# A fused mLSTM-attention and MLP kernel: from the fourth chunk a step's weighing and the next step's scores become one block on TensorE, with a cheaper set-up and a new table of order

## The chip, the cores and the metric

The kernel runs on one core of a Trainium2 chip. The metric is the device time of one launch in microseconds. The inputs lie in HBM in a layout that the host prepared; everything below happens in one program on the core's engines: PE (TensorE, matmuls and transposes), DVE (VectorE), ACT (ScalarE), POOL (GpSimd) and SP (SyncE, which here only issues DMAs).

## The reference, cut to what matters

```python
# attention, per batch and head (4 batches x 8 heads, 768 tokens, head size 40)
for t in range(S):
    m_new  = max(f_gate[t] + m, i_gate[t])
    f_stab = exp(f_gate[t] + m - m_new);  i_stab = exp(i_gate[t] - m_new);  m = m_new
    C = f_stab * C + i_stab * outer(v[t], k[t])
    n = f_stab * n + i_stab * k[t]
    y[t] = sigmoid(o_gate[t]) * (C @ q[t]) / max(abs(n . q[t]), 1.0)
# MLP on the 3072 tokens (320 wide, 2048 hidden)
x = y laid out as 3072 x 320
h = x @ w_in
g = h * erf(softplus(h))
return g @ w_out
```

All data is float32. Products of the MLP are made from high and low halves (three products for most of `h`, three for most of the output), so that TensorE's faster float32 form keeps enough bits.

## The kernel before, in words

**Tiling.** The 768 tokens are cut into 12 chunks of 64. A chunk has two *steps*, r = 0 and r = 1, each of two of the four batches with all their heads. The matrix C and the vector n live in `state[r]`, one tile for each r, which a chunk's step reads and then updates. After both steps of a chunk its 256 rows of y are transposed and go through the MLP in four *groups* `mlp(g)`, 48 in all: each group takes 512 of the 2048 hidden units.

**A step on PE** has these blocks, all into `pa` tiles in PSUM, of which there are two: *scores* (L626, k times q, 16 matmuls in the program); *state part* (L635, `qe` times `state`); *key/value part* (L640, the addition to the state); *heads* (L649, the weighted scores `dm` times v, which ends the step's output). In the program the scores, the state part and the heads are 16, 16 and 32 instructions; the trace counts each of them twice. The transposes of the chunk before (L510, three for each step) share the scores' tile. From chunk `JOIN` = 3 on, one planned operation holds transposes, state part, key/value part and scores; the heads come later as an operation of their own, when DVE has multiplied the scores into `dm` (L681). Behind the heads DVE makes the divisor (L710 to L712), the output (L718, L724), a copy of 64 columns of it that the third transpose needs (L725), and the new state (L730, L732).

**A group on PE**: 32 up matmuls into two `h` tiles (L858, products `xh,wh`, `xl,wh` and for two thirds `xh,wl`), later the down matmuls into the two halves of `pob`: L915 for the first six groups, which are not split, and L917, L919 and L920 for the others. Between them ACT copies h (L866), runs softplus and erf (L870, L874) with a change of its table before each (L985), and DVE multiplies (L878) and forms the low half `gl` (L894). When the four groups of a chunk are summed up, ACT copies each half of `pob` to `o` (L925), from where it is stored. The next chunk's first down matmuls write the same `pob` tile, and wait for that copy.

**Opening.** POOL makes masks and constants (`one`, `ident`, `keep`, L347 to L384) and `sel` (L362 to L370), which says for each partition which gate it holds. DVE's first instruction (`heads_of`, L379) and ACT's work on `one` (L375) need `sel`. DVE then runs the gate scans (L432 to L450) and splits the weights as they arrive (L740, L751, L753, L767, L805). The inputs qk, kvo, w_in (two halves of 512 KB each for several parts), w_out and the gates are issued by SP.

**What sets the order.** All operations are handed to a `Plan`, which lists them with costs and due times (`FIRST_DUE`, `EVERY`, `STEPS`, plus a table `SHIFT` with a number for each operation) and replays them with a model of the engines; on each engine the ready operation with the earliest due time is next. The resulting order is the program's order, engine by engine; waits are only for data and for buffers. The model also counts PE's instructions in blocks of `BLOCK`, and holds up an operation that would cross into a block before `FETCH` microseconds have gone by; where it foresees a gap on PE it puts in filler matmuls on `ident` (`stay`, L983).

## Time and profile before

| what | us |
|---|---|
| runs before, median (lowest to highest), 3 runs | 481.37 (480.41 to 481.48) |
| the profiled execution | 479.99 |
| its span (first to last instruction) | 478.3 |
| mean granted clock of TensorE | 0.993 |
| last output copy starts | 474.28 |

The profiled execution is 1.7 us longer than its span, and 1.38 us shorter than the median of the runs. In the lines of the profile, times are microseconds from the span's start. "L858" is line 858 of the kernel before; "[0.53 <-ACT o L925]" means that the engine stood idle for 0.53 us, and that the last thing it waited for was ACT's instruction of that line. "x8" is the number of instructions drawn into one row; "128*128" is the part of the array that a matmul uses. In the windows view a row gives, for each engine, its busy time in the stretch and the number of instructions, then the granted clock, the busy share of the DMA engines and the bytes that they moved.

### The profile page before, as it was taken

The numbers are of one execution on the slowest core, as the hardware profiler recorded it, in microseconds if no ns is written. First come the engines' busy times: TensorE is split into PE (matmuls) and PEld (weight loads), VectorE is DVE, ScalarE is ACT, GpSimd is POOL, SyncE is SP. The second block draws the span as 40 slices with busy tenths as digits, with TensorE's granted clock in tenths as the row PEclk, the third lists the DMA queues.
The fourth block names the chain that finished last, engine by engine and source line by source line (L and its number), as shares of the span: only waits on it lengthen the run. The fifth ranks groups of instructions, "written<-read, shape, count | busy, mean of one in ns | idle before, by whom it ended". The sixth has DMA issues, their size and how long they took to land.

```text
span 478.3 us, 14687 instructions
## 1 busy us (share of the span) xinstructions
PE 456.3 (95%) x6482; PEld 421.5 (88%) x6482; DVE 322.0 (67%) x574; ACT 313.6 (66%) x433; POOL 48.2 (10%) x71
## 2 busy tenths in 40 slices
PE   6788999899999999999999999999999999999996
PEld 2457878678999999999899999999999999999985
DVE  4889999999988378367639557769069551554280
ACT  3636799948598399648179288396287272894760
POOL 4000002101203003002101101104003100000000
PEclk9979999999999999999999999999999999999999
DMA  8997835332362433033324313604040300000011
GB/s 282 313 307 224 270 123 170 105 116 78 115 169 66 134 128 129 18 116 107 93 108 128 104 29 108 171 14 143 7 127 21 116 16 1 2 14 15 1 27 29
DMA packets 42476, 50.77 MB, mean 106 GB/s; under 512 B 22700, under 2 KB 27308, under 8 KB 42412
## 3 DMA queue, kind: packets, MB, share of 16 engines
q1 hardware_dynamic: 42412, 49.83, 34.6%
q8 instruction: 51, 0.84, 0.7%
q14 instruction: 13, 0.11, 0.1%
HBM read 45.68 MB, written 4.13 MB: 104 GB/s over the span
## 4 chain that ended last, share of the span: by engine, by line
PE 82%; DVE 8%; ACT 7%; issue 2%; POOL 1%; POOLq 0%; ACTq 0%; DVEq 0%
PE h L858 35%; PE pob L919 10%; PE pob L917 10%; PE pob L920 9%; PE pa L649 3%; PE pob L983 3%; PE pa L635 2%; PE pa L626 2%; PE pob L915 2%; PE pa L915 2%; ACT L985 2%; DVE raw L751 1%; PE pa L510 1%; PE pa L640 1%; ACT n L870 1%
## 5 line engine op out<-in xcount | busy, mean ns | idle before, releaser
L858 PE MATMUL h<-xh,wh 128*128 128x256 f32 x576 | 159.6, 288 | 0.0
L858 PE MATMUL h<-xl,wh 128*128 128x256 f32 x576 | 156.7, 283 | 0.0
L858 PEld LDWEIGHTS h<-xh,wh 128*128 128x128 f32 x576 | 110.0, 191 | 1.9 <-ACT hb L866 0.6
L858 PEld LDWEIGHTS h<-xl,wh 128*128 128x128 f32 x576 | 110.2, 191 | 0.7 <-DVE vg L614 0.2
L866 ACT ACTIVATE hb<-h 128x512 f32<-128x512 f32 x96 | 56.4, 593 | 81.9 <-PE h L858 81.8
L858 PE MATMUL h<-xh,wl 128*128 128x256 f32 x384 | 108.6, 283 | 0.1
L919 PE MATMUL pob<-woh,gh 128*128 128x320 f32 x328 | 99.4, 315 | 1.6 <-ACT o L925 1.6
L920 PE MATMUL pob<-wo,gh 128*128 128x320 f32 x328 | 97.5, 309 | 0.0
L878 DVE TENSOR_TENSOR n<-n,hb 128x1024 f32<-128x1024 f32 x48 | 58.7, 1231 | 40.9 <-ACT n L874 40.8
L985 ACT ACT_TABLE_LOAD x61 | 78.3, 1283 | 1.8 <-PEq L1038 0.8
L604 POOL TENSOR_SCALAR_AFFINE_SELECT dm<-dm 128x512 f32<-128x512 f32 (+1 forms) x40 | 42.5, 1069 | 322.6 <-ACT dm L583 321.3
L858 PEld LDWEIGHTS h<-xh,wl 128*128 128x128 f32 x384 | 73.4, 191 | 0.3 <-DVE wl L767 0.3
L919 PEld LDWEIGHTS pob<-woh,gh 128*128 128x128 f32 x328 | 61.6, 188 | 3.5 <-ACT o L925 2.4
L917 PE MATMUL pob<-woh,gl 128*128 128x320 f32 x328 | 61.0, 314 | 1.8 <-ACT o L925 1.6
L920 PEld LDWEIGHTS pob<-wo,gh 128*128 128x128 f32 x328 | 61.6, 188 | 0.0
L894 DVE TENSOR_TENSOR gl<-n,gh 128x1024 fp32r<-128x1024 f32 x42 | 52.1, 1245 | 2.0 <-ACT gh L888 1.0
L917 PEld LDWEIGHTS pob<-woh,gl 128*128 128x128 f32 x328 | 50.4, 188 | 3.4 <-ACT o L925 2.4
L870 ACT ACTIVATE n<-hb 128x1024 f32<-128x1024 f32 x48 | 50.6, 1058 | 1.2
L874 ACT ACTIVATE n<-n 128x1024 f32<-128x1024 f32 x48 | 49.5, 1053 | 0.2
L710 DVE TENSOR_SCALAR den<-pa 128x8 f32<-128x8 f32 x24 | 3.9, 161 | 46.8 <-PE pa L649 45.8
L925 ACT ACTIVATE o<-pob 128x320 f32<-128x320 f32 x22 | 9.3, 435 | 32.6 <-PE pob L917 26.3
L681 DVE TENSOR_TENSOR dm<-pa,dm 128x512 f32<-128x512 f32 x24 | 16.5, 687 | 20.0 <-PE pa L626 17.3
(94 smaller groups left out, 537.0 us busy)
## 6 DMA issues: line engine op xcount, KB each, us to landing
qk<-in_qk_dram SPq DMA_DIRECT2D x24, 512.0 KB
kvo<-in_kvo_dram SPq DMA_DIRECT2D x24, 484.0 KB
raw<-in_w_out_dram SPq DMA_DIRECT2D x16, 320.0 KB
dm<-gd SPq DMA_DIRECT2D x40, 128.0 KB
raw<-in_w_in_dram SPq DMA_DIRECT2D x8, 512.0 KB
out_dram<-o SPq DMA_DIRECT2D x48, 80.0 KB
eT<-gd SPq DMA_DIRECT2D x22, 128.0 KB
eT<-gd SPq DMA_DIRECT2D x22, 80.0 KB
```

What stands on the lines that cost most here:

```text
L604: nc.gpsimd.affine_select(out=x, in_=x, pattern=[[0, H], [1, L]], compare_op=ALU.is_ge, fill=0.0, base=base, channel_multiplier=-1)
L858: nc.tensor.matmul(h[:, n * T:(n + 1) * T], w, m, start=(s == 0), stop=(s == len(ops) - 1))
L866: nc.scalar.activation(G('hb')[:, hs], G(f'h{i}'), AF.Copy)
L870: nc.scalar.activation(new('n0', [128, 1024], ('n0', g)), G('hb'), AF.Softplus)
L874: nc.scalar.activation(G('n0'), G('n0'), AF.Erf)
L878: nc.vector.tensor_tensor(G('n0'), G('n0'), G('hb'), op=ALU.mult)
L894: nc.vector.tensor_tensor(new('gl', [128, 1024], ('gl', g), F32R), G('n0'), G('gh').bitcast(F32), op=ALU.subtract)
L915: nc.tensor.matmul(acc(b), G('n0')[:, ts], t['wo', j], start=(j == 0), stop=(j == NFF - 1))
L917: nc.tensor.matmul(acc(b), G('gl')[:, ts], woh[:, j], start=False, stop=(j == NFF - 1))
L919: nc.tensor.matmul(acc(b), G('gh')[:, ts], woh[:, j], start=(j == 0), stop=False)
L920: nc.tensor.matmul(acc(b), G('gh')[:, ts], t['wol', j], start=False, stop=False)
L985: order = plan.run(lambda k: nc.scalar.preload_act_table_set(KIND[k]), stay)
```

## The change: what it does

**One block in place of two.** From chunk `PIPE` = 3 on, `run(r, step)` puts into one planned PE operation: the transposes of step r of the chunk before, then the whole weighing of the step before (state part, key/value part, heads), then the scores of step r. So r = 0 of a chunk carries the weighing of r = 1 of the chunk before (kept in `pending`), and r = 1 carries that of r = 0. There are 18 such operations with scores, 17 of them with a weighing; the last weighing stands by itself. `post(r)` has DVE's work behind the heads, `mult(r)` the product of scores and `dm`; both hold what they held, in an order that fits.

**Blocks of instructions.** `BLOCK` goes from 634 to 640, `FETCH` from 5.0 to 4.4, the model starts at 157.5 of a block, and a fetch is taken to begin `LEAD` = 160 instructions ahead of a block's end (it began at the boundary). `WIDE_FILL` goes from 0.85 to 0.65.

**Set-up.** `sel` is computed by DVE from `cst` and a mask `own`, which POOL makes without waiting for a load; POOL reads `one`'s blocks from a tile `zero` in place of clearing each. The eight POOL instructions of `sel` become five of DVE.

**The copy of 64 columns** that the third transpose needs goes from DVE to ACT (`ACT_TWICE`), 24 times.

**Order.** `FIRST_DUE`, `EVERY`, `LAG`, `STEPS` and the whole table `SHIFT` have new numbers, and the gates' first load is due early.

```diff
-    BLOCK, FETCH, SPREAD, SAME = 634, 5.0, 8.0, 1.0
+    BLOCK, LEAD, FETCH, SPREAD, SAME = 640, 160, 4.4, 8.0, 1.0
...
     def fetch(self, now, cost, mm):
 
-        at, begun = self.block
-        while at + mm >= self.BLOCK:
-            n = self.BLOCK - at
-            now = max(now + cost * n / mm, begun + self.FETCH)
-            cost, mm, at, begun = cost * (mm - n) / mm, mm - n, 0, now
+
+        at, begun, mark = self.block
+        while True:
+            lim = self.BLOCK - self.LEAD if at < self.BLOCK - self.LEAD else self.BLOCK
+            if at + mm < lim:
+                return now + cost, (at + mm, begun, mark)
+            n = lim - at
+            if mm:
+                now, cost, mm = now + cost * n / mm, cost * (mm - n) / mm, mm - n
+            at = lim
+            if lim < self.BLOCK:
+                mark = now
+            else:
+                late = begun + self.FETCH > now
+                now = max(now, begun + self.FETCH)
+                begun, at = now if late else mark, 0
             if not mm:
-                break
-        return now + cost, (at + mm, begun)
+                return now + cost, (at, begun, mark)
...
-EVERY = 8.133349751406488
+EVERY = 7.861941783669311
...
+ACT_TWICE, PIPE = True, 3
...
-    @op('POOL', 1.3, r=[('cst', 0)], w=[('is', 0)], due=-70.0)
+    @op('DVE', 0.7, r=[('cst', 0), ('own', 0)], w=[('is', 0), ('hd', 0)], due=-70.0)
     def _():
-        nc.gpsimd.tensor_tensor(sel[:, 1:2], cst[:, 9:10], cst[:, 8:9], op=ALU.subtract)
...
+        nc.vector.tensor_tensor(sel[:, 1:2], cst[:, 9:10], cst[:, 8:9], op=ALU.subtract)
...
+            if ACT_TWICE:
+                @op('ACT', 0.24, w=[K('kvo', r, 'o')])
+                def _(r=r):
+                    nc.scalar.activation(A('kvo', r)[:, KV + 320:KV + 384], A('kvo', r)[:, KV + 256:KV + 320], AF.Copy)
...
+            @op('PE', cost, r=reads, w=writes, tile_=tiles, kind='a', mm=mm, after=after)
+            def _():
+                if r is not None:
+                    new('pa', [128, 1024], ('S', c, r))
+                    if was:
+                        turned(*was, A('S', r)[:, 256:256 + 3 * W])
+                if step is not None:
+                    step.weigh()
+                if r is not None:
+                    scores(r)
+
+        if c >= PIPE:
...
+            for r, step in enumerate([pending[0], steps[0]]):
+                run(r, step)
+                if step is not None:
+                    step.post()
+                if prev is not None:
+                    divided(prev, {r: ('S', c, r)})
+                mult(r)
+            pending[0] = steps[1]
+            if last:
+                run(None, steps[1])
+                post(1)
+            return
```

**What stands in a row on PE, in the steady part.** Before, in the middle of the fourth chunk's groups, the operation with the transposes is followed by down matmuls, and the heads stand apart among ups:

```order
L510 MATMUL pa<-ident,kvo 128x128 x3
L635 MATMUL pa<-state_71,qe 64x41 x16
L640 MATMUL pa<-vg,kvo 64x41 x2
L640 MATMUL pa<-vg,kvo 40x41 x2
...
L626 MATMUL pa<-qk 64x64 x16
L919 MATMUL pob<-woh,gh 128x320
L920 MATMUL pob<-wo,gh 128x320
```

Of the change, at the corresponding place (lines 527, 655, 660, 669, 646 are what 510, 635, 640, 649, 626 were, 945 is 858):

```order
L527 MATMUL pa<-ident,kvo 128x128 x3
L655 MATMUL pa<-state_74,qe 64x41 x16
L660 MATMUL pa<-vg,kvo 64x41 x2
L660 MATMUL pa<-vg,kvo 40x41 x2
...
L669 MATMUL pa<-kvo,dm 32x41 x32
L646 MATMUL pa<-qk 64x64 x16
L945 MATMUL h<-xh,wh 128x256
```

The heads stand between the key/value part and the scores now. In the rows left out of both are six more of the key/value part. The block of heads among ups that went with the first piece is this, where L858 are ups:

```order
L858 MATMUL h<-xh,wh 128x256
L858 MATMUL h<-xl,wh 128x256
L649 MATMUL pa<-kvo,dm 32x41 x32
L858 MATMUL h<-xh,wh 128x256
L858 MATMUL h<-xl,wh 128x256
```

This row apart is gone from the changed kernel's fourth chunk on.

**At the output copy, on PE.** Before, about 43% of the way through the program, eight low-half down matmuls (L917) close a chunk's sum, and the next chunk's down matmuls (L919, L920) stand right behind:

```order
L858 MATMUL h<-xh,wh 128x256
L858 MATMUL h<-xl,wh 128x256
L917 MATMUL pob<-woh,gl 128x320 x8
L919 MATMUL pob<-woh,gh 128x320
L920 MATMUL pob<-wo,gh 128x320
```

In the changed kernel at such a place (L1004, L1006, L1007 are what L917, L919, L920 were) ups follow the eight:

```order
L1006 MATMUL pob<-woh,gh 128x320
L1007 MATMUL pob<-wo,gh 128x320
L1004 MATMUL pob<-woh,gl 128x320 x8
L945 MATMUL h<-xh,wh 128x256
L945 MATMUL h<-xl,wh 128x256
```

Before there were six places where the first write of `pob` behind a closing L917 waits with no other matmul between that write and the matmul that releases the copy; in the changed kernel there are two, both close to the end of the program, and elsewhere at least 16 ups or a whole attention block lie between.

**SP at the start.** Before, its first DMAs are:

```order
L343 DMA cst<-in_consts_dram 128x12
L553 DMA qk<-in_qk_dram 128x2x512
L423 DMA gt<-in_gates_dram 128x2x128
L775 DMA raw<-in_w_in_dram 128x1024
L557 DMA kvo<-in_kvo_dram 128x968 x2
L553 DMA qk<-in_qk_dram 128x2x512
```

In the changed kernel:

```order
L361 DMA cst<-in_consts_dram 128x12
L900 DMA raw<-in_w_out_dram 128x640
L440 DMA gt<-in_gates_dram 128x2x128
L573 DMA qk<-in_qk_dram 128x2x512
L900 DMA raw<-in_w_out_dram 128x640
L862 DMA raw<-in_w_in_dram 128x1024
L577 DMA kvo<-in_kvo_dram 128x968
L878 DMA raw<-in_w_in_dram 64x1024 x2
L862 DMA raw<-in_w_in_dram 128x1024 x2
L517 DMA gd_209<-x 8x4x64 x4
L878 DMA raw<-in_w_in_dram 64x1024 x2
L577 DMA kvo<-in_kvo_dram 128x968 x2
L573 DMA qk<-in_qk_dram 128x2x512 x2
```

The second step's `qk` was sixth, and the list up to it and with it held 2638 KB; now it is the first of the last row's two, and the list up to it and with it holds 5842 KB.

More of the change, by code (lines that the diff above doesn't have):

```diff
@@ L512, in divided @@
     def divided(c, keys):
[L513 removed]
+        for r, key in keys.items():
+            key = (key, 'p')
             ts = slice(r * W, (r + 1) * W)
@@ new lines, in mult, with _, weigh @@
+        def mult(r):
+            plan.part = f'a{c}{r}'
+            @op('DVE', 0.64, r=[K('S', r)], w=[K('dm', r)])
+            def _():
+                s = ends(A('S', r)).rearrange("p j (n t) -> p j n t", t=L)
+                nc.vector.tensor_tensor(dm(r), s, dm(r), op=ALU.mult)
+        def weigh(r):
+            if r == 0:
+                for n in ('xh', 'xl'):
+                    new(n, [128, 3, T], (n, c), F32R)
+            new('pa', [128, 1024], ('ph', c, r))
+            before(r)
+            heads(r)
```

142 lines of the change are left out of this document (83 added, 59 removed).

## The prediction

> **What bounds the kernel now.** I read the page's busy times first, then PE's waits, then the windows by stage. The page:
>
> ```profile
> PE 456.3 (95%) x6482; PEld 421.5 (88%) x6482; DVE 322.0 (67%) x574; ACT 313.6 (66%) x433; POOL 48.2 (10%) x71
> ...
> q8 instruction: 51, 0.84, 0.7%
> ```
>
> PE is busy for 95% of the span; no other engine comes near. So the time is PE's work plus PE's holes, and the windows say where the holes are:
>
> ```profile
> 0.00:12.00 12.00, 7.72 (x14) 3.45 (x15) 5.41 (x17) 3.87 (x7) 5.71 (x31) 1.00 0.83 282
> 12.00:24.00 12.00, 9.25 (x297) 5.38 (x295) 9.66 (x20) 7.79 (x14) 0.00 (x0) 1.00 1.02 313
> 24.00:36.00 12.00, 10.35 (x62) 6.14 (x63) 10.08 (x23) 4.38 (x10) 0.00 (x0) 0.72 1.08 307
> ...
> 60.00:84.00 24.00, 23.07 (x199) 19.66 (x199) 22.84 (x41) 23.60 (x38) 2.84 (x4) 1.00 0.47 146
> 84.00:98.00 14.00, 11.64 (x299) 9.53 (x298) 13.28 (x36) 11.69 (x21) 1.44 (x2) 1.00 0.26 87
> ...
> 116.00:474.50 358.50, 354.88 (x5141) 344.26 (x5139) 221.33 (x356) 232.01 (x300) 36.56 (x32) 1.00 0.26 76
> ```
>
> The columns are the window, its length, busy time of PE, PEld, DVE, ACT, POOL, the granted clock, the DMA share and GB/s. Two regimes: to about 98 us PE idles or runs fillers while DMA (share about 1 to 36 us), ACT (23.60 of 24 from 60 to 84) and DVE (13.28 of 14 from 84 to 98) are full; from 116 us PE is busy 354.88 of 358.50. What PE waits for in the two:
>
> ```profile
> PE pa L635 <- DVE state L732: 1.0, 1, 1.0
> PE pa L626 <- DVE dm L681: 0.8, 1, 0.8
> PE pob L915 <- issue: 0.8, 1, 0.8
> PE pob L915 <- DVE wo L753: 0.6, 1, 0.6
> ```
>
> These are all of PE's waits of note from 72.5 to 98.5 us; and from 98.5 us to the end:
>
> ```profile
> PE pob L917 <- ACT o L925: 1.6, 3, 0.5
> PE pob L919 <- ACT o L925: 1.6, 3, 0.5
> PE pob L917 <- DVE gl L894: 0.2, 1, 0.2
> ```
>
> So the change can win from three places: the opening, six waits on the output copy, and what PE's work itself costs by its order. The steady part has 3.4 us of waits in all, hence no large gain is to be had there.
>
> **1. The opening.** DVE begins late, because it waits for `sel`:
>
> ```profile
> 6.07 0.29 DVE L379 TENSOR_SCALAR heads_of<-cst,sel 128x8 f32<-128x8 f32 x1 [6.07 <-POOL sel L365]
> ...
> 6.33 0.48 DVE L432 TENSOR_TENSOR_SCAN m<-gt,m 128x128 f32<-128x128 f32 x1
> ```
>
> POOL makes it behind its masks. On DVE, `sel` needs `cst` (6 KB, first in SP's list) and one mask. I estimate the scan at 5.0 in place of 6.33, 1.3 us sooner. Bounds: no gain, if the gates' load (128 KB, behind 320 KB of w_out now: 0.32 MB at the row's 282 GB/s is 1.1 us) holds the scan; 2 us if nothing does. The copies that leave DVE in the opening are four, and this row, from 20 to 75 us, gives each one's least, median and longest in ns:
>
> ```profile
> L725 DVE COPY kvo<-kvo x4: 195/195/195, 22.3 to 47.8; 128x64 f32<-128x64 f32 x4
> ```
>
> 4 × 0.195 = 0.8. So DVE's lead at 60 us is between 1.3 and 2.1, and I take the middle, **−1.7**, for ACT's full stretch that hangs on it. ACT gets the copies; it was busy 4.38 of 12 just before, so they hide there; without that cover 4 × 0.2 = 0.8 comes back. In the steady part ACT gets the other 20 copies, 4 us in 358.50 of which it is busy for 232.01: nothing; DVE loses as much, also at no gain.
>
> Against this stands SP's new order. The second step's `qk` is complete behind 5842 KB, about 6.0 MB: 3.4 MB in the first 12 us at 282 GB/s and 2.6 MB at 313 is 8.3 more, so about 20.4 us; before, 2638 KB at 282 is 9.6 us. The first up matmul will be late for that:
>
> ```profile
> 33.99 0.68 PE L858 MATMUL h<-xh,wh 128*128 128x256 f32 x1
> ```
>
> In the list of DVE's instructions, some 9 us more stand ahead of what the first up needs: one more step's output, a state update and more weight splits. Before, DVE had 5.41 + 9.66 us in the first two windows and about 7.8 of the third's 10.08 behind it at the first up, some 22.9; with nine more that is 31.9 (an estimate), so with a start at 5.0 the first up comes at 36.9, three us later (bounds 35.5 if DVE starts still earlier, 39 if it idles 2 us for loads). But this is chunk 1's attention done early: what PE and DVE do ahead of the first up is not left to do behind it, and the ups that it delays find their weights split. I therefore cost the swap at 0, bounds −2 and +2.
>
> **2. Waits from 72.5 to 98.5.** The four rows above sum to 3.2 us. Three are on DVE's results (state, dm, wo) in a stretch where DVE is full; with DVE ahead by 1.3 to 2.1 us, more than the longest of them (1.0), they go. The fourth is an instruction fetch (part 5). I take all four, **−3.2**; bounds 0 (new ones in their place) and −3.2. What is late next there is ACT, busy 11.69 of 14.
>
> **3. The output copy.** One of the six places, on PE:
>
> ```profile
> 204.92 0.28 PE L858 MATMUL h<-xl,wh 128*128 128x256 f32 x1
> 205.04 1.33 PE L917 MATMUL pob<-woh,gl 128*128 128x320 f32 x8
> 206.89 0.41 PE L919 MATMUL pob<-woh,gh 128*128 128x320 f32 x1 [0.53 <-ACT o L925]
> ```
>
> Eight matmuls start every 0.146 us (1.33 less the last one's 0.31, by seven), so 1.17 of the 1.85 us between the starts is work and 0.68 is lost. The order shows that in four of the six places at least 16 ups (16 × 0.12 = 1.9 us) or an attention block (2.6 us) now lie between, more than the 0.68. 4 × 0.68 = **−2.7**. Bounds: −1.4, if ACT's queue makes two of them wait anyway; −4.1, if all six go.
>
> **4. The merge itself.** The heads apart among ups:
>
> ```profile
> 126.64 0.28 PE L858 MATMUL h<-xh,wh 128*128 128x256 f32 x1
> 126.76 0.28 PE L858 MATMUL h<-xl,wh 128*128 128x256 f32 x1
> 126.97 0.81 PE L649 MATMUL pa<-kvo,dm 64*32 64x41 f32 x64
> 127.71 0.39 PE L858 MATMUL h<-xh,wh 128*128 128x256 f32 x1
> 127.93 0.28 PE L858 MATMUL h<-xl,wh 128*128 128x256 f32 x1
> ```
>
> An up takes 0.12 (126.76 less 126.64), so from 126.76 to 127.93 the heads cost 1.17 − 0.24 = 0.93. The other operation:
>
> ```profile
> 131.52 0.28 PE L858 MATMUL h<-xl,wh 128*128 128x256 f32 x1
> 131.73 0.68 PE L635 MATMUL pa<-state,qe 40*64 40x41 f32 x32
> ...
> 132.68 0.66 PE L626 MATMUL pa<-qk 40*64 40x64 f32 x30
> 133.27 0.39 PE L858 MATMUL h<-xh,wh 128*128 128x256 f32 x1
> 133.49 0.28 PE L858 MATMUL h<-xl,wh 128*128 128x256 f32 x1
> ```
>
> 1.97 − 0.24 = 1.73; together 2.66. What the merged one costs is read from chunk 1, where state part, key/value part and heads already stand in a row:
>
> ```profile
> 38.10 0.28 PE L858 MATMUL h<-xl,wh 128*128 128x256 f32 x1
> 38.31 0.68 PE L635 MATMUL pa<-state,qe 40*64 40x41 f32 x32
> ...
> 39.37 0.81 PE L649 MATMUL pa<-kvo,dm 64*32 64x41 f32 x64
> 40.11 0.63 PE L481 MATMUL pa<-ident,x 128*128 128x32 f32 x4
> ```
>
> 38.10 to 40.11 less one up is 1.89; plus the scores, 0.59 for 30 passes or 0.63 for 32; plus the late start of the second up behind such a block, 127.93 − 127.71 − 0.12 = 0.10. That is 2.62, 0.04 less than apart. 17 × 0.04 = **−0.7**. The pair apart enters and leaves the block's array shape twice; the gain is no larger, since heads to scores is a change of shape too (64*32 to 40*64). Bounds: 0 and −17 × 0.2 = −3.4, if one of the two entries (0.21 at 126.97, against 0.12) with its bump went wholly.
>
> The Trainium skill, "TensorEngine Tiling (Array Packing)", section "Key Properties", says that a change of tiling mode drains the array. Counted so, there are four changes before and four after, and merging by itself gives nothing; the rows agree to 0.04 us.
>
> The merged operation takes both `pa` tiles, so the next step cannot start until DVE has emptied the heads' one: seven instructions (L710 to L732), which at 0.2 to 0.7 us by the DVE rows above are under 5 us. The order leaves at least 6 us of PE work between two of them: 0, at most 1 us for a few.
>
> **5. Instruction fetch.** The page counts 51 packets of PE code (16 KB each). A merged operation is 166 passes in 2.6 us, short matmuls in a row, so code is used up fastest there. Twice before PE stood on "issue" right behind such a dense row:
>
> ```profile
> 21.93 0.74 PE L649 MATMUL pa<-kvo,dm 64*32 64x41 f32 x57 [0.43 <-issue]
> ```
>
> and
>
> ```profile
> 94.72 1.07 PE L915 MATMUL pob<-wo,n 128*128 128x320 f32 x3 [0.80 <-issue]
> ```
>
> with a code packet moved from 92.0 to 93.5:
>
> ```profile
> q8 instruction: 1, 0.02, 3.9%
> ```
>
> Both are behind one of the six steps of chunks 0 to 2, which are not split: two stalls in six, 0.6 us on average. The 17 merged steps are as dense. At the same rate 17 × 2/6 × 0.6 = 3.4 us; but two packets within 187.5 to 191.5 did no harm:
>
> ```profile
> q8 instruction: 2, 0.03, 3.2%
> ```
>
> I take four stalls of 0.6, **+2.4**; bounds 0 and +3.4 (all 17 is a rival below).
>
> The Trainium skill, "Runtime: NRT & Kernel Launch", section "Instruction fetch mechanics", says that code comes in 16 KiB blocks and that crossing into the next is mostly hidden. By that rule this term is 0; the two rows on "issue" speak against it for dense rows.
>
> **The sum.** Against the profiled execution (479.99, span 478.3; the tail from the last copy at 474.28 stays): −1.7 − 3.2 − 2.7 − 0.7 + 2.4 = −5.9, so 474.1. The median of the runs shown lies 1.38 above that execution; on it, 481.37 − 5.9 = **475.5**.
>
> **The rivals.**
> - *Fetch is hidden.* The 187.5 row is for it, the issue rows against. Without the term: 473.1.
> - *The opening gives more.* DVE's holes of the first 36 us (12 − 9.66 and 12 − 10.08 in the windows) go as well, the first up comes at 35.5 and the swap is worth its bound of −2, and fetch is partly hidden: about 472.
> - *The opening gives nothing.* The gates land behind w_out, `qk` lands at 20.4, ACT's stretch starts no earlier, and the waits of part 2 stay. Then −2.7 − 0.7 + 2.4 = −1.0: 480.4; with the swap at its +2, 482.4. For it: DMA's share is about 1 to 36 us.
> - *Slower: a fetch stall in every merged step.* Each has at least one block boundary in its 166 passes with their weight loads (332 instructions against 256), so 17 stalls of 0.80, the longer row, are 13.6; with the gains of 8.3 that is +5.3, 486.7. It decides from 8.3 / 0.8, some ten stalls. Against it: four of the six unsplit steps had none.
>
> **How the numbers follow.** The measurement tells about 0.2%, 1.0 us, from no change. Forecast 0.45; fetch hidden 0.2; opening better 0.1; opening nothing 0.14 (of it 0.06 faster, 0.06 same, 0.02 slower); slower by fetch 0.11. Faster is 0.45 + 0.2 + 0.1 + 0.06 = 0.81, same 0.06, slower 0.13. The range: below, 475.5 less fetch (2.4), the swap (2) and the last two copies (1.4) is 469.7, so 469.5; above, the opening's 4.9 and one more us of fetch on 475.5 give 481.4, so 481. Left out are the rival at 486.7 and some of the opening's bad end.
>
> **What would show it right or wrong.** Right: `heads_of` or the scan at about 5; first up near 36.9; no wait of DVE's over 0.5 us on PE from 72 to 98; two waits of 0.53 on the output copy; merged blocks of 2.6 us; a few issue rows of 0.4 to 0.8 right behind them. Wrong: issue rows at ten or more merged blocks; PE waiting for a `pa` tile (DVE's state or output) ahead of the merged blocks; ACT's full stretch from 60 us starting no sooner; new waits on weights between 40 and 70.

## The result, and the profile after

The changed kernel takes 488.85 us in the median (487.19 to 490.81), beside 481.43 us of the kernel before on the same chip (480.41 to 483.35): a ratio of **1.0148**, interval 1.0118 to 1.0178. It is slower by 1.5%, where the prediction was 475.5 and its range ended at 481. The profiled execution took 488.81 us, with a span of 487.1 and a mean granted clock of 0.974 (before: 478.3 and 0.993).

PE's row of the page:

```profile
PE 463.2 (95%) x6480; PEld 428.5 (88%) x6480; DVE 318.8 (65%) x555; ACT 317.8 (65%) x457; POOL 43.8 (9%) x63
```

PE is busy for 6.9 us more over as many instructions, and its share is 95% again. So the share tells nothing; part of the loss hides inside "busy". The windows by stage (columns as in the prediction: length, busy of PE, PEld, DVE, ACT, POOL, granted clock, DMA share, GB/s) show where:

```profile
24.00:36.00 12.00, 9.76 (x297) 7.66 (x301) 7.76 (x20) 3.33 (x7) 0.00 (x0) 0.57 1.09 336
36.00:60.00 24.00, 21.99 (x267) 18.58 (x268) 19.47 (x44) 13.53 (x28) 0.00 (x0) 0.79 0.55 198
...
84.00:98.00 14.00, 14.00 (x115) 11.73 (x114) 13.45 (x28) 12.67 (x24) 3.02 (x4) 1.00 0.22 78
...
116.00:474.50 358.50, 350.88 (x5115) 342.22 (x5115) 217.15 (x341) 234.78 (x320) 34.10 (x32) 1.00 0.27 78
```

The same view of the kernel before had, from 36 to 60 us:

```profile
36.00:60.00 24.00, 21.43 (x388) 19.12 (x387) 22.45 (x51) 16.71 (x28) 0.00 (x0) 1.00 0.83 248
```

From 24 to 36 us DVE is busy for 7.76 us (10.08 before) at a clock of 0.57 (0.72), from 36 to 60 for 19.47 (22.45) at 0.79 (1.00), while PE is busy just as long; from 84 to 98 PE has no hole at all (11.64 of 14 before); from 116 it is busy 350.88 of 358.50 (354.88 before). PE's waits in the changed kernel (us in total, times, longest; "issue" stands where the profile shows nothing that PE waited for), in three fences: up to 72 us (a wait of 4.0 us for `ident` at the start, 4.3 before, is left out), from 72 to 98, and behind:

```profile
PE pa L646 <- DMA qk<-in_qk_dram: 2.2, 2, 1.7
PE pa L646 <- issue: 1.5, 1, 1.5
PE pa L655 <- issue: 1.4, 1, 1.4
```

```profile
PE h L945 <- ACT hb L953: 0.5, 1, 0.5
```

```profile
PE pa L498 <- DVE state L714: 2.4, 1, 2.4
PE pa L646 <- issue: 1.3, 1, 1.3
PE h L945 <- DVE xl L541: 1.1, 2, 0.7
PE h L945 <- ACT hb L953: 1.1, 1, 1.1
PE pob L1006 <- ACT o L1012: 1.1, 2, 0.6
PE pa L655 <- DVE m L448: 0.5, 1, 0.5
PE pob L1004 <- ACT o L1012: 0.5, 1, 0.5
PE h L945 <- issue: 0.5, 1, 0.5
```

The middle list is what the change gained: 0.5 us where four waits had summed to 3.2. The first and the last are what it paid. The waits on the output copy are three of 0.5 to 0.6, not six.

The orders differ, so the same time means different work. I therefore compare at equal work: every PE instruction except fillers counts at its undisturbed spacing (an up 0.120 us, an output matmul 0.147, the short ones 0.012 to 0.019), which sums to 424.9 us in every kernel here; the time at which PE reaches a given work, less that work, is what has been lost so far. Worked out from the traces:

```
lost by PE (us) at work done of     40     60    100    400   100 to 400
kernel before (73.6, 98.6, 139.1,  33.6   38.6   39.1   46.8     7.7
               446.9 us)
changed kernel                     39.9   40.3   44.5   55.6    11.1
e1 later qk loads                  44.2   44.6   50.4   60.5    10.1
e2 earlier qk load                 39.3   39.7   45.7   53.1     7.4
e3 92 instructions more            47.3   47.7   54.0   63.9     9.9
e4 before, with the set-up         33.0   37.6   38.3   45.9     7.6
e5 order of before to 100 us       34.3   39.0   43.9   51.7     7.8
e6 gates' matmuls later            41.6   42.0   48.5   60.0    11.5
e8 e5, seam mended                 33.3   39.1   41.5   50.0     8.5
e9 e8, 12 instructions fewer       31.9   35.8   39.3   45.5     6.2
e12 e9, order of before to 118 us  31.3   35.3   42.9   48.6     5.7
e13 changed, 12 instructions fewer 39.8   40.2   46.2   53.6     7.4
e14 e12, seam mended               33.0   36.9   39.8   45.8     6.0
e15 e14, one copy moved            33.6   37.6   38.4   45.2     6.8
```

Read the second row against the first: **+6.3 in the opening, −4.6 from there to 98 us, +3.7 to some 140 us, +3.4 in the steady part.** The end is 8.8 later. Each row is one execution, the profiled one. These lie from 1.6 us below the median of their runs (e4) to 4.2 above it (e6); the kernel before is 1.4 below, so between the medians the 8.8 are 7.4. The opening of one and the same code varies too: e6 is the changed kernel up to 121 us, and differs by 1.7 at 40 us of work.

### The profile page after: what moved, and what is told of

Read it like the earlier page. It is cut to its first block, busy times and chain, and to the rows that moved or that the text cites. A ratio compares the mean times of both kernels' runs of the same rounds, so it can differ in the third digit from the quotient of the medians.

```text
span 487.1 us, 14685 instructions
## 1 busy us (share of the span) xinstructions
PE 463.2 (95%) x6480; PEld 428.5 (88%) x6480; DVE 318.8 (65%) x555; ACT 317.8 (65%) x457; POOL 43.8 (9%) x63
## 4 chain that ended last, share of the span: by engine, by line
PE 65%; DVE 13%; ACT 11%; DMA 5%; issue 4%; SPq 1%; DVEq 0%; ACTq 0%
PE h L945 30%; PE pob L1006 9%; PE pob L1007 8%; PE pob L1004 8%; DMA raw<-in_w_in_dram 3%; ACT L1072 3%; PE pa L669 3%; PE pa L655 2%; DVE n L965 2%; PE pa L646 2%; ACT n L957 2%; ACT n L961 2%; PE pa L660 2%; DMA qk<-in_qk_dram 2%; ACT hb L953 1%
## 5 line engine op out<-in xcount | busy, mean ns | idle before, releaser
L1006 PE MATMUL pob<-woh,gh 128*128 128x320 f32 x328 | 99.1, 314 | 1.1 <-ACT o L1012 1.1
L1007 PE MATMUL pob<-wo,gh 128*128 128x320 f32 x328 | 98.0, 311 | 0.0
L624 POOL TENSOR_SCALAR_AFFINE_SELECT dm<-dm 128x512 f32<-128x512 f32 (+1 forms) x40 | 40.1, 1011 | 333.5 <-ACT dm L603 296.3
L1006 PEld LDWEIGHTS pob<-woh,gh 128*128 128x128 f32 x328 | 62.2, 190 | 2.0 <-ACT o L1012 1.6
L1007 PEld LDWEIGHTS pob<-wo,gh 128*128 128x128 f32 x328 | 62.3, 190 | 0.0
L1004 PE MATMUL pob<-woh,gl 128*128 128x320 f32 x328 | 60.2, 313 | 0.6 <-ACT o L1012 0.5
L1004 PEld LDWEIGHTS pob<-woh,gl 128*128 128x128 f32 x328 | 51.1, 190 | 1.3 <-ACT o L1012 0.8
L617 DVE TENSOR_TENSOR qe<-qk,eT 104x512 f32<-104x512 f32 x22 | 16.1, 733 | 19.0 <-PE pa L655 10.4
L722 DVE TENSOR_TENSOR dm<-pa,dm 128x512 f32<-128x512 f32 x18 | 12.3, 686 | 18.5 <-PE pa L646 15.9
```

The costliest lines, as they stand in the source:

```text
L617: nc.vector.tensor_tensor(new('qe', [128, 2, NPR, L], ('qe', c, r))[0:CR], A('qk', r)[0:CR, :, 0], A('eT', r)[0:CR], op=ALU.mult)
L624: nc.gpsimd.affine_select(out=x, in_=x, pattern=[[0, H], [1, L]], compare_op=ALU.is_ge, fill=0.0, base=base, channel_multiplier=-1)
L1004: nc.tensor.matmul(acc(b), G('gl')[:, ts], woh[:, j], start=False, stop=(j == NFF - 1))
L1006: nc.tensor.matmul(acc(b), G('gh')[:, ts], woh[:, j], start=(j == 0), stop=False)
L1007: nc.tensor.matmul(acc(b), G('gh')[:, ts], t['wol', j], start=False, stop=False)
```

## The experiments

All orders below are the kernel's own lists with operations moved; dependencies and buffers stay as they are.

**e1: are the early `qk` loads in the way of the code packets?**

```diff
+    parts = {'a20:SP', 'a21:SP', 'a30:SP'}
+    rest = [x for x in order if x not in late]
+    return rest[:at + 1] + late + rest[at + 1:]
```

> The changed kernel with three loads that nothing needs before 75 us (qk of chunk 2, both steps, and of chunk 3, first step: 1.5 MB) issued behind the second gate block's stores (53 us) instead of at 26 to 32 us; every other engine's order is kept. Theory A (code packets wait behind data: 2.4, 3.8 and 4.0 us from the start of a code block to its successor's packet while the DMA share is over 1, against 0.5 to 1 us later): the data stream ends near 37 us instead of 41, the packets at 35.70 and 42.01 come sooner, the first up moves from 44.8 to about 41 to 42.5, and the time falls by 2 to 4 us, to 485 to 487. Theory B (the opening is set by the late second qk and DVE's list, and the stalls on code only fill a wait that is there anyway): first up 44.3 to 45, time within 1 us of 488.9.

Measured: 491.7 (ratio 1.0213, 1.0183 to 1.0243), slower than both theories had it. The first up came at 50.31 us. One stall alone, from PE's timeline of e1 (start, length, instruction, idle time before it):

```profile
37.29 0.34 PE L665 MATMUL pa<-state,qe 40*64 40x41 f32 x3 [4.94 <-issue]
```

Other loads fill the same time (in e1 the DMA share is 1.10 from 32 to 36 us), and the code packet that ends this stall starts at 34.57 us only. Putting these three loads off is no cure.

**e2: is the second step's `qk` what makes the opening late?**

```diff
+    rest = [x for x in order if x is not qk[0] and not (isinstance(x[2], int) and x[2] == 5 and x[0] < 20)]
+    return rest[:at + 1] + qk + rest[at + 1:]
```

> The changed kernel with the second step's qk issued right behind the first step's kvo (seventh place on SP in place of fifteenth), and without the five filler matmuls that stood ahead of its scores. Theory B1 (the late qk sets the opening): the second step's scores start at about 18 instead of 24.39, and the first up comes 5 us or more sooner, 40 or less; time down by 5 us or more, to 484 or less. Theory B2 (DVE's list, with nine more us ahead of the first up, and the code set it): the scores start at 18, but what follows waits for DVE's output of the first step, which ends at 23.8 as before; first up between 42 and 45, time within 2 us of 488.9.

Measured: 487.81 (1.0135, 1.0091 to 1.018), theory B2 by its time; first up at 46.2, no sooner than in the changed kernel. The scores that need this `qk` start at 19.95 in place of 24.39, but PE waits for something else instead, as its waits up to 72 us in e2 show:

```profile
PE pa L538 <- ACT wh L899: 5.5, 1, 5.5
```

These are the transposes of the first step's output, which they read from `kvo`; the view puts the wait down to ACT's weight split, but DVE's last write of `kvo` ends only at 25.97 us (23.80 in the changed kernel). It stands behind weight splits in DVE's list, and these start later here, for the w_in loads moved back when `qk` moved up (DVE waits 1.76 us for one). So this one load is not the cause; what stands ahead in the other engines' lists holds PE next. That the loads as a whole cost nothing, e2 does not show. The five fillers left out are 20 instructions, and the loss from 100 to 400 us of work fell from 11.1 to 7.4: e13 comes back to that.

**e3: code alignment alone, the wrong way.**

```diff
-        for _ in range(n):
-            if accs:
+        for _ in range(28 if n == 5 and not accs else n):
+            if n == 5 and not accs:
+                nc.tensor.matmul(pob[:, 1, 0:16], ident, ident[:, 0:16], start=True, stop=True)
+            elif accs:
```

> The changed kernel with the five fillers of 512 columns at 18 us replaced by 28 of 16 columns: 92 more instructions (23 more matmuls, two passes each, each with a weight load) ahead of everything that follows, so that all later boundaries of 256 instructions lie 92 instructions earlier in the work. If the stalls at 213.8, 353.0 and 369.3 come from a boundary pair inside a merged step (a block used up in 2.8 to 5.1 us), they leave these three places, and other merged steps may stall: between 100 and 480 us between one and six stalls of 0.5 to 1.5 us at other places, time within 3 us of 488.9. If they come from the work at these places (ACT's hb at 213.8, as the profile has it, or the merged step itself), they stay there within 0.3 us. In the opening the stalls at 30.5, 36.5 and 44.2 change too.

Measured: 496.94 (1.0326, 1.0296 to 1.0355). The narrow fillers took 11.1 us themselves (19.97 to 31.06), where the five wide ones had taken 4.56, so the time says little. The places say more: the stalls at 213.8, 353.0 and 369.3 us were gone, and others stood at 231.73, 327.08 and 342.52, in or right behind other merged blocks. Counted in the matmuls of PE's trace, the three old ones stand 81, 74 and 74 behind a multiple of 128, the three new ones 81, 75 and 75, and 128 matmuls with their weight loads are the 256 instructions of a code block. A stall belongs to where these boundaries fall, not to the work there.

**e4: the shorter set-up alone, in the kernel before.**

```diff
-        nc.gpsimd.tensor_tensor(sel[:, 1:2], cst[:, 9:10], cst[:, 8:9], op=ALU.subtract)
...
+        nc.vector.tensor_tensor(sel[:, 1:2], cst[:, 9:10], cst[:, 8:9], op=ALU.subtract)
```

> The kernel before, with the set-up of the change alone (sel on DVE, own and zero on POOL), in the order of before. By the prediction's term (DVE's scan 1.3 us sooner, ACT's full stretch sooner): scan at 4.8 to 5.1 instead of 6.33, time down by 0.5 to 1.5 us, to 480 to 481. Rival (the opening is held by loads and by ACT, not by the start of DVE): the scan comes sooner, the first up stays at 33 to 34, and the time within 0.5 us of 481.4.

Measured: 480.72 (0.998, 0.9956 to 1.0003); the first up 0.6 us sooner, the end 0.9. DVE's first scan, in the timeline of e4:

```profile
5.49 0.48 DVE L438 TENSOR_TENSOR_SCAN m<-gt,m 128x128 f32<-128x128 f32 x1 [1.55 <-DMA gt<-in_gates_dram]
```

It waits for the gates' load here, the bound that the prediction had named; in the changed kernel, which issues that load earlier, the scan starts at 4.79. By this row the set-up is worth some 0.6 to 0.9, but two executions of one kernel differ by as much, and the interval reaches 1.0003. What e4 does show are PE's waits from 72 to 98 us, in the order of before:

```profile
PE pa L641 <- DVE state L738: 0.9, 1, 0.9
PE pa L632 <- DVE dm L687: 0.8, 1, 0.8
PE pob L921 <- DVE wo L759: 0.7, 1, 0.7
```

The three waits on DVE that DVE's lead was to remove are all still there, with a lead of 0.84 us (6.33 to 5.49).

**e5: the old order to 100 us, the changed kernel's behind it.**

```diff
+SEQ = [('s', 'X'), 2, 3, 0, 21, 9, 135, 7, 22, 1, 8, 6, ('f', 6), 4, ...]
-        return [fn for _, fn in order]
+        order = edit(order)
+        return [x[1] for x in order]
```

`SEQ` lists the operations by number, `f` a run of fillers, `s` a table load.

> The changed kernel, with the instructions that it plans up to about 100 us put in the order of the kernel before; behind that its own order, with the merged blocks and the output matmuls as changed. Theory A: the new order of the opening costs its whole loss at the 161st up matmul (6.4 us at equal work) and nothing of it comes back later, so 488.9 - 6.4 = 482.5, with the first up at about 33.4 and the 161st at about 72; less 1 us if the instruction block at 121.62's wait falls better. Theory B: the loss is PE work and clock that is merely moved (the stretch from 72 to 98 us gains 4.9 in the change, and this gain goes with the old opening), so little changes: 486 to 489. The stalls at block boundaries near 213.8, 353 and 369 us stay in both, since the later code is only 4 instructions off.

Measured: 485.62 (1.0089, 1.006 to 1.0117), between the theories. The opening's loss is gone (34.3 at 40 us of work), but 4 us came anew at 115 to 122 us, from the seam, the place where the old order gives way to the new one: DVE stood for the fifth pair's gates, which share one buffer with the pair just read, and PE behind it for `gh` (2.28 us, with 3.4 us of half clock behind it). e8 puts that load and its scan behind both runs of `gl`:

```diff
-874, ..., 875, 289, 306, 290, 274, 876, 307, ..., 291, 1072
+874, ..., 289, 306, 290, 274, 307, ..., 291, 875, 876, 1072
```

> e5 with one mend of its seam at 100 us: there DVE waited 1.05 us for the gates of the fifth pair (they share one buffer with the third pair's, which DVE had just read), and PE then 2.28 us for gh, with half a clock behind it. The fifth pair's load and DVE's scan of it now stand behind both gl. Theory A (the opening is the whole difference up to 131 us, and e5's 4 us came from that seam): 485.6 less 2.3 for the wait and 1.8 for the half clock, 481.5, with no PE wait over 1 us between 100 and 125 us. Theory B (from the fourth chunk the order asks more of DVE than it can do by 120 us, whatever the opening is): another wait takes its place and the time stays at 484 to 486.

Measured: 484.64 (1.0071, 1.0043 to 1.0098), theory B's time. PE's waits from 98 us in e8:

```profile
PE h L968 <- ACT n L984: 1.6, 1, 1.6
PE pa L1029 <- ACT gh L998: 1.3, 1, 1.3
```

The wait for `gh` went from 2.3 to 1.3 us and the half clock behind it is gone, so that 2.4 us less are lost at 100 us of work. At 400 us of work 1.7 of them are left: the hole near 210 us is longer (1.57, the upper row, against 1.22 in e5), and it is a code stall, as e9 shows. The medians differ by 1.0 only.

**e6: is the wait of 2.4 us at 121.62 a cost of its own?** The two matmuls of the gate block (679) and ACT's copies (680) are moved 63 places back:

```diff
-383, 315, 495, 384, 386, 679, 385, 296, 680, 585
+383, 315, 495, 384, 386, 385, 296, 585
...
+410, 494, 299, 679, 680, 421
```

> The changed kernel, with the two matmuls of the gate block that wait 2.4 us at 121.6 us for DVE's state, and ACT's copies of them, placed some 14 us further back in the order. Theory A: the wait is a cost of its own (PE stands in front of a pa tile that DVE has not read yet, with ready ups behind): 2.4 us go, 488.9 - 2.4 = 486.5, and the ups move ahead. Theory B: DVE is simply late there, and what comes next needs the same tiles, so the wait passes to the transposes behind (L527): 487.7 to 488.9.

Measured: 489.02 (1.0168, 1.0107 to 1.023), theory B. PE's waits from 98 to 140 us in e6:

```profile
PE pa L692 <- issue: 1.8, 1, 1.8
PE pa L550 <- DVE state L737: 1.2, 1, 1.2
```

Half of the wait passed to the next operation that needs a `pa` tile, the transposes, and a code stall appeared at 131 us. DVE was late, not the gates. (This profile is of an execution of 493.18 us, 4.2 above the median; the rows tell where the wait went, not what it costs.)

**e7 and e10: how fast does PE get its code?** Both leave out the whole computation. e7 took too long a matmul (106 ns each, 13.6 us per 256 instructions) and showed no stall in either half: at that pace the code comes in time, and what short matmuls do stays open. e10 has those.

```diff
-            nc.tensor.matmul(acc[0:64, 0:41], a[0:64, 0:64], b[0:64, 0:41], start=True, stop=True)
+            nc.tensor.matmul(acc[os, 0:41], a[ds, 0:32], b[ds, 0:41], start=True, stop=True)
```

> Leaves out the whole of the reference's computation (the output is zeros) and only measures instruction fetch: 960 short fp32 matmuls in a row without other transfers, then 960 more while 24 loads of 484 KB each run. Theory A: the packet of the next 256 instructions starts about half a microsecond behind the start of the block before and is usable 1.2 to 1.6 us after it has landed, so that dense short matmuls take about 3 us per 256 instructions without other transfers, and 5 to 6.5 us beside the loads, as in the opening (packets 2.4 to 4 us after the block's start there). Theory B: the opening's stalls have another cause than the transfers: the time per 256 instructions is the same in both halves.

> Leaves out the whole of the reference's computation (the output is zeros) and only measures instruction fetch: 2560 matmuls of the heads' kind (64x32 by 64x41, four places of the array in turn; 128 of them, with their weight loads 256 instructions, are 1.5 us of work) without other transfers, then 2560 more with 24 loads of 484 KB beside the first of them. Theory A: without loads 256 instructions take about 3.05 us, since the packet of the next 256 starts half a microsecond behind the block before, takes 1.0 and is usable 1.4 later; beside the loads 5 to 6.5 us, as in the opening. Theory B: the fetch runs ahead by more than one block, and 256 instructions take near 1.5 us without loads; the steady stalls then have another cause.

e10's windows, without loads and with them (columns: length, busy of PE, PEld, ACT, POOL, clock, DMA share, GB/s):

```profile
20.00:60.00 40.00, 26.48 (x1408) 24.74 (x1408) 0.00 (x0) 0.00 (x0) 0.50 0.02 5
...
152.00:176.00 24.00, 8.94 (x485) 8.46 (x488) 0.00 (x0) 0.00 (x0) 0.52 1.02 406
```

The trace of e10 has 20480 matmuls and weight loads and 80 code packets, 256 to a packet; that of the changed kernel 12960 and 51, 254 to a packet. In e10 PE stands still after every 128th matmul. 40 × 128 / 1408 = 3.64 us per 256 without loads, 24 × 128 / 485 = 6.3 with them, the latter as theory A had it. The former is above its 3.05: the clock is 0.50 here, and the packet starts later behind its block, 1.0 to 1.7 us in the packets' records, not half a microsecond. (Why the clock stays at 0.50 was not tried.) By those records a packet takes about 1.0 and its code starts 1.2 to 1.6 us after its end, in both halves; at the three stalls of the changed kernel's steady part it is 1.27, 1.38 and 1.50. Beside the loads the packet starts 3.3 to 4.8 us behind its block. So while PE works on one block, no more than the next one is on its way.

The Trainium skill, "Runtime: NRT & Kernel Launch", section "Instruction fetch mechanics", calls the crossing into the next block mostly hidden; in e10 it is not, by 1.0 to 1.6 us of idle PE in every block of short matmuls without loads, and 3.8 to 5.0 beside them, while in e7 it is.

**e9 and e13: the alignment.** Three early fillers less are 12 instructions less ahead of all else; e9 does it to e8, e13 to the changed kernel.

```diff
-22, 1, 8, 6, ('f', 6), 4, 28
+22, 1, 8, 6, ('f', 3), 4, 28
```

```diff
-7, 4, 6, 8, 22, ('f', 3), 5, 126
+7, 4, 6, 8, 22, 5, 126
```

> e8 with three of the six fillers at the start of PE's work left out: 12 instructions fewer ahead of everything, so that every block of 256 begins 12 instructions later in the program. Theory A (a stall stands where two block boundaries fall into one attention block, less than 3.05 us apart): the stalls near 212 us (1.2) and, smaller, 351 and 367 us (0.6 and 1.0) go down to about 1.0 in sum, and the half clock that follows a stall over 1 us with them: 2 to 3 us less than e8. Theory B (those stalls are waits for ACT or DVE, as the profile names the one at 213 us): they stay, and e9 is within 1 us of e8.

> The changed kernel with three early fillers left out and nothing else: 12 instructions fewer ahead of the rest (these fillers stand at the start, before PE waits for the second step's qk at 22.65 us, so their time itself brings nothing). Theory A (two block boundaries in one attention block): the stalls at 213.8, 353.0 and 369.3 us (1.14, 0.47, 1.25) shrink to about 1.0 in sum, and the half clock behind the last (1.7) goes: 488.9 - 1.9 - 1.7 = 485.3. Theory B (waits for ACT or DVE): 488 to 490.

Measured: e9 480.21 (0.9978, 0.9955 to 1.0001), 4.4 below e8; of that 2.3 lie between 100 and 400 us of work (8.5 to 6.2), the rest ahead of that, where PE's wait on "issue" fell from 2.4 to 0.8 us. e13 488.37 (1.0163, 1.0105 to 1.0221): by its total theory B, by its rows theory A. PE's waits from 98 us in e13:

```profile
PE pa L521 <- DVE state L737: 2.4, 1, 2.4
PE pa L692 <- issue: 1.5, 1, 1.5
```

The issue stalls at 353 and 369 us shrank to under 0.4, the hole at 213 from 1.14 to under 0.4, and the loss from 100 to 400 us went from 11.1 to 7.4, the 3.6 of theory A. But a new stall of 1.53 stands at 129.4, in a merged block that had none, with 1.7 us more lost up to 100 us of work. Alignment is worth 2 to 4 us in these rows, and has to be right everywhere: the medians of e13 and the changed kernel differ by 0.5.

What theory B had for itself was this row of the changed kernel's timeline of PE:

```profile
213.79 0.28 PE L945 MATMUL h<-xh,wh 128*128 128x256 f32 x1 [1.14 <-ACT hb L953]
```

with ACT's own timeline:

```profile
212.52 0.24 ACT L707 ACTIVATE kvo<-kvo 128x64 f32<-128x64 f32 x1
212.69 0.60 ACT L953 ACTIVATE hb<-h 128x512 f32<-128x512 f32 x1
```

`hb` was done at 213.29, half a microsecond before the up. A code packet ended at 212.52, and 1.27 us later is 213.79. About half of the hole is ACT, the last part is code, and the profile names only ACT.

**e11: what does a hole do to the clock?**

```diff
+    holes = [], [8], [256], [512], [512, 128], [512, 512], [512] * 3, [512] * 4, [512] * 6
```

> Leaves out the whole of the reference's computation (the output is zeros) and only measures the clock: stretches of 13 to 16 us of matmuls of the ups' kind, and between them holes of about 0.5 to 4.5 us in which PE waits for ACT, each size four times. Theory A (a hole costs a half clock behind it): holes of 2 us and more are all followed by some 3.4 us at half clock (1.7 us more than the hole), holes under 1 us by none, and those of 1.2 to 2 us by chance of where they fall. Theory B: single holes of up to 4 us leave the clock at 1.00, and the half clock in the changed kernel's opening comes from the low share of PE's work over 20 us or more.

Two of its holes of 2.38 us, at 104.08 and 248.84 (columns: length, busy of PE, PEld, ACT, POOL, clock, DMA share, GB/s):

```profile
106.00:108.00 2.00, 1.55 (x13) 1.55 (x14) 0.40 (x2) 0.00 (x0) 1.00 0.00 0
...
250.00:252.00 2.00, 0.79 (x4) 0.79 (x5) 1.13 (x3) 0.00 (x0) 0.87 0.00 0
252.00:254.00 2.00, 2.00 (x12) 2.00 (x11) 0.00 (x0) 0.00 (x0) 0.50 0.00 0
254.00:256.00 2.00, 2.00 (x15) 2.00 (x15) 0.00 (x0) 0.00 (x0) 0.78 0.00 0
```

The first cost nothing more; the second cost 2 × (0.13 + 0.50 + 0.22) = 1.7 us of work behind it, which is 3.4 us at half clock. Of four holes of 2.38 us two did so, of four of 3.04 two (those at 421.00 and 583.00), of three of 4.36 all, of twenty of 0.57 to 1.71 none. Theory A had said all from 2 us up, theory B none: it is a matter of where the hole falls. By the trace's clock records the half clock starts at 138.83, 251.47, 289.01, 405.06, 425.55, 442.61 and 585.97 us, apart by whole multiples of 3.413, and lasts one such window or two. With the time cut into these windows, all nine in which PE, with work still to come, stood for 1.90 us or more (up to 3.08) are followed by one at half clock, and none of those with 1.85 or less is. So in this dense work a hole of 4.36 always costs it (half of it is 2.18), one of 1.71 never, and one between by its place. In the changed kernel it took less, a code stall of 1.25 us at 369.34 inside a merged block of short matmuls (columns as in the prediction):

```profile
368.00:370.00 2.00, 0.75 (x11) 0.60 (x6) 0.30 (x1) 2.00 (x4) 0.00 (x0) 1.00 0.00 0
370.00:372.00 2.00, 2.00 (x10) 2.00 (x9) 1.90 (x7) 1.97 (x3) 0.00 (x0) 0.50 0.04 8
372.00:374.00 2.00, 2.00 (x11) 2.00 (x10) 1.96 (x2) 1.98 (x5) 1.47 (x2) 0.65 0.67 155
```

2 × (0.50 + 0.35) = 1.7 us again: the stall cost 2.9, not 1.25. So the idle time is not all that counts; what makes short matmuls weigh less was not tried.

The Trainium skill, "TensorE: Matmul & The Clock Gate", section "Part 1: The HAM clock gate (the "warmup" mystery)", tells of a free-running window of about 3.4 us and half the clock after an idle one. The 3.4 us, the windows' own pace and the role of chance agree with e11; a window need not be idle throughout, since 1.90 us of it in dense work, or 1.25 in a merged block, were enough.

**e12, e14, e15: the stretch from 107 to 139 us.** e12 keeps the order of before to 118 us:

```diff
-SEQ = [('s', 'X'), 2, 3, 0, 21, 9, 135, ...]
+SEQ = [('s', 'X'), 2, 3, 0, 21, 9, 135, ..., 336, 875, 876, 1072, 679, 680, 1073, 293, 297, ...]
```

> e9 with the order of the kernel before kept up to about 118 us of its plan and not only to 100; behind that the changed kernel's own, with the merged blocks. At equal work PE lost 2.9 us between 107 and 139 us in e9 and 0.5 in the kernel before. Theory A (the new order behind the opening brings PE to gates and state that DVE has not got to): with the old order to 118 us this goes, 480.2 - 2.4 = 477.8, under the kernel before. Theory B (DVE is short of time up to about 120 us in any order, so that PE waits in one place or the other): 480 to 481, the wait shows up behind 118 us.

Measured: 483.44 (1.0032, 1.0009 to 1.0055), above both. From 122.59 us PE stood for 4.58 us (its timeline in e12):

```profile
127.17 1.06 PE L692 MATMUL pa<-kvo,dm 64*32 64x41 f32 x49 [4.58 <-DVE dm L745]
```

and DVE's timeline, in front of that `dm`:

```profile
125.96 0.49 DVE L472 TENSOR_TENSOR_SCAN m<-gt,m 128x128 f32<-128x128 f32 x1 [2.01 <-DMA gt<-in_gates_dram]
126.36 0.67 DVE L745 TENSOR_TENSOR dm<-pa,dm 128x512 f32<-128x512 f32 x1
```

The scan waits for its load at the head of DVE's list, with the result that PE needs right behind it. This is again the seam, so e14 puts scans and load behind both runs' `dm`:

```diff
-336, 875, 876, 1072, 679, 680, 1073, 293, ..., 477, 582, ..., 497, 493
+336, 679, 680, 293, ..., 477, 875, 876, 1072, 582, ..., 497, 1073, 493
```

> e12 with its seam mended: there DVE stood 2.01 us at 123.95 us in front of a scan that waits for the next pair's gates (one buffer, read only just before), with the first run's dm behind it, for which PE waited 4.58 us at 122.59 and then ran 8 us at half clock. The two scans and the load now stand behind the dm of both runs. Theory A (the new order's loss between 107 and 139 us in e12 is this seam): the wait and the half clock go, 483.4 - 4.6 - 1.8 = 477.0, at most 478.5. Theory B (DVE is short of time there in any order): PE still waits 2 us or more for dm or state between 118 and 140 us, and the time is 480 to 482.5.

Measured: 479.64 (0.9963, 0.9943 to 0.9984), between the theories and under the kernel before, 3.8 of theory A's 6.4 us gained. The wait for `dm` was gone, and another stood at 131.45: PE for `hb`, 1.81 us. ACT's timeline there:

```profile
130.33 0.26 ACT L730 ACTIVATE kvo<-kvo 128x64 f32<-128x64 f32 x1 [7.15 <-DVE kvo L723]
130.49 0.42 ACT L1035 ACTIVATE o<-pob 128x320 f32<-128x320 f32 x1
130.81 0.59 ACT L976 ACTIVATE hb<-h 128x512 f32<-128x512 f32 x1
```

This is one of the 24 copies that the change gives to ACT: 0.26 us of work that stood 7.15 us at the head of the list, and two evictions behind it. e15 moves that copy behind them:

```diff
-493, 475, 298, 408, 407, 295, 595, 419, 409, 410
+493, 298, 408, 407, 295, 595, 419, 409, 475, 410
```

> e14 with one instruction moved: ACT's copy of 64 columns (L729 of its code, one of the 24 that the change gives to ACT), which stood 7.15 us at the head of ACT's list at 130.33 us waiting for DVE's kvo, goes behind the two evictions of hb that follow it. PE waited 1.81 us at 131.45 for the first of these. Theory A (the copy in ACT's list, and nothing else, holds the ups up): 479.6 - 1.8 = 477.8. Theory B (ACT or DVE is short of time there anyway, and the merged block behind waits as long for the same copy): 479.0 to 480.0.

Measured: **477.47** (ratio **0.9913**, 0.9898 to 0.9928), as theory A said to 0.3 us. PE's waits from 98 us in e15:

```profile
PE h L968 <- DVE xl L564: 1.2, 2, 0.7
PE pob L1029 <- ACT o L1035: 1.1, 2, 0.5
...
PE h L968 <- issue: 0.5, 1, 0.5
```

None is over 0.7 us any more. This is the changed kernel, with its merged blocks, copies and set-up; it differs in the order of its first 118 us, in the places of the scans and their load (e14) and of one copy (e15), and by three fillers (e9). It beats both kernels.

## Why the prediction was wrong, point by point

On the profiled executions the sum missed by 14.7 us (488.81 against 474.1): by 6.6 up to 98 us (−4.9 forecast, +1.7 measured), by 3.7 from there to 140 us (0 forecast) and by 4.4 in the steady part (−1.0 forecast, +3.4 measured).

**The opening: "I therefore cost the swap at 0, bounds −2 and +2."** This is the step that failed first, and cost most. Measured: the first up at 44.83 in place of an estimated 36.9, and 6.3 us lost at 40 us of work; with the set-up's 0.6 to gain (e4), the swap cost some 7. I had counted the work ahead of the first up on DVE alone, as if DVE never stood (2 us at the bound of 39). The start was right, with the scan at 4.79, and so was the work: from there to the first up DVE is busy for 32.32 us, near the forecast's 31.9. But DVE also stands for 7.7 of these 40.0 us. The second `qk`, too, let PE go on only at 24.39, not at 20.4: I had counted the bytes ahead of it, and SP issues it at 17.89 only. Two steps of attention in a row are a chain through all engines: from 24 to 60 us DVE waited, by its waits in the changed kernel,

```profile
DVE den L686 <- PE pa L669: 1.9, 1, 1.9
...
DVE den L686 <- ACT state L680: 1.2, 1, 1.2
...
DVE dm L801 <- PE pa L646: 0.8, 2, 0.6
DVE state L714 <- PE pa L669: 0.8, 1, 0.8
```

for PE's results and ACT's, while PE ran at a clock of 0.57 and 0.79 or stood for code or data. DVE's 10.08 + 22.45 = 32.5 busy us of before became 7.76 + 19.47 = 27.2. That the order is the cause, e5, e8 and e15 show: with the old one the loss at 40 us of work is 33.3 to 34.3, as before. That it is not the load of `qk` alone, e2 shows. A better clock alone does not help either: from 20 to 60 us the mean granted clock is 0.74 in the changed kernel and 0.87 in e13, and both reach 40 us of work within 0.1 us, for in e13 longer holes take its place (4.0 us for DVE's `lt`, 3.0 on code). Which engine's list does it, and what part the loads have, was not tried apart.

**"What PE and DVE do ahead of the first up is not left to do behind it."** This held: 4.6 of the 6.3 us came back by 98 us, and with them went the waits of part 2. But the sum took that gain as its own (−3.2) beside a swap of 0, where it was the swap's return. Part 2 was thus near in number (0.5 left of 3.2) by luck. Its reason, DVE's lead, is not borne out: the set-up alone (e4) leaves the three waits on DVE at 0.9, 0.8 and 0.7, and set-up and copies together in the old order (e5) leave them at 0.9, 0.8 and 0.6.

**The `pa` tiles: "0, at most 1 us for a few."** Too low: at 121.62 PE waited 2.42 us for DVE's last reading of one, at 110.3 another 0.5. I had measured the distance between two merged blocks in PE work and the seven DVE instructions at their own length, without what stands ahead of them in DVE's list. e6 shows that it is DVE that is late; e12 and e14, that one DVE instruction waiting at the head of the list is enough. That no such loss need be there, e15 shows: 0.8 from 60 to 100 us of work, beside 4.2.

**The output copy: four of six places, −2.7.** Three went, at 0.7 each some −2: the step was right, the size short by one place.

**The merge: 2.62 us.** From PE's timeline in the changed kernel's steady part:

```profile
140.51 0.68 PE L655 MATMUL pa<-state,qe 40*64 40x41 f32 x32
...
142.31 0.69 PE L646 MATMUL pa<-qk 40*64 40x64 f32 x32
142.94 0.38 PE L945 MATMUL h<-xh,wh 128*128 128x256 f32 x1
143.16 0.28 PE L945 MATMUL h<-xl,wh 128*128 128x256 f32 x1
```

State part, key/value part, heads and scores take 2.43 (142.94 − 140.51), and 143.16 − 142.94 − 0.12 = 0.10 behind, just what rows of chunk 1 gave. By these rows the −0.7 stands; no run tried the merge alone.

**Instruction fetch: four stalls of 0.6, +2.4.** In the steady part there were three (0.47, 1.25, and a part of 1.14), close in number and in sum; what the sum left out is the half clock behind one (1.7), and the opening, where code has to come through full DMA queues (1.5 and 1.4). The rival that lies nearest in time, 486.7 with a stall in every merged block, is wrong all the same: three of 17 have one, in or right behind a block at whose end a second boundary falls (the matmuls that stall are the last but one of it, the second behind it and the 17th behind it).

**ACT's 24 copies: "nothing".** Wrong in kind: I looked at ACT's busy share. In e14 one cost some 2 us by its place in the list (1.81 of wait; 479.64 to 477.47 when it moved). In the changed kernel one stands right ahead of the late `hb` at 212.69; what it costs there was not tried.

The steady part adds up roughly: stalls 2.9, half clock 1.7, new waits on `xl` 1.1, the output copies −2.0 (three of the six lie between 100 and 400 us of work), the merge −0.7: +3.0 of 3.4.

## What to carry to other kernels

A new order is a change on every engine's list at once: cost each instruction by what stands ahead of it on its own engine, and ask of each that can wait (a scan for a load, a copy for another engine) who stands behind it. Compare two orders at equal work, not at equal time; a gain at one place was here the return of a loss at another. Before a change is thrown out, run parts of it in the old order: with the first 118 us of before and the three small mends of e9, e14 and e15 this one is 0.9% faster, and as it came it is 1.5% slower.

## What the runs showed of the hardware

- Code reaches PE in blocks of 256 instructions (20480 over 80 packets in e10); a block's code is usable 1.2 to 1.6 us after its packet has ended, and the packet starts only when PE has been in the block before for 1.0 to 1.7 us, 3.3 to 4.8 beside loads. Short matmuls ran at 3.6 us per 256 at half clock, at 6.3 beside loads at 406 GB/s (e10).
- The granted clock changes on a grid of 3.413 us (e11; in the changed kernel half clock starts at 25.26, 38.91 and 370.00 us, 4 and 97 steps apart). In e11's dense work a window with 1.90 us of idle PE or more was followed by one at half clock (nine of nine), one with 1.85 or less never; holes of 2.4 to 4.4 us gave it in seven of eleven cases. A hole of 1.25 us between short matmuls gave it too, and where such matmuls pause for 1.0 to 1.6 us every 3.6 us, the clock stays at 0.50 (e10).
- The profile puts a wait down to the engine whose semaphore came last, also where the code came later still (213.79).
